# Forty zero matmuls from the start instead of fifteen later ones, a new order of all steps, and q loaded ahead of k, in a linear-attention and MLP-mixer kernel

## The chip, the cores and the metric

The kernel runs on one core of a Trainium2 chip. The metric is device time in microseconds (us). The core has a matrix engine (TensorE, PE in the profile; PEld are its weight loads), a vector engine (VectorE, DVE), a scalar engine (ScalarE, ACT), a general engine (GpSimd, POOL) and a sync engine (SyncE, SP) that issues almost all transfers. Each engine works off its own list of instructions in order; they wait for each other through semaphores. Transfers from SP are served by 16 DMA engines, behind each other in one queue (q1 in the profile); the ScalarE queue (q10) issues one load at the start and three stores at the end.

## The reference

Eight batches of eight heads, 576 tokens, 64 values per head. Linear attention with a cosine weighting of the position gives x, in which the heads stand side by side (512 channels); a token MLP (576 to 256 to 576) works across the tokens, and a channel MLP (512 to 1536 to 512) across the channels.

```python
def phi(x, c, s):
    r = np.maximum(x, 0.0)
    return np.concatenate([r * c, r * s], axis=-1)
q_p, k_p = phi(q, cos_w, sin_w), phi(k, cos_w, sin_w)
kv  = np.einsum('bhsf,bhsd->bhfd', k_p, v)
z   = np.sum(k_p, axis=2)
num = np.einsum('bhsf,bhfd->bhsd', q_p, kv)
den = np.einsum('bhsf,bhf->bhs', q_p, z)[..., None] + 1e-06
x   = num / den                                   # as [B, S, H * D]
xt  = x.transpose(0, 2, 1)
h   = np.maximum(xt @ w_tok1, 0.0) @ w_tok2
u   = x + h.transpose(0, 2, 1)
out = u + np.maximum(u @ w_ch1, 0.0) @ w_ch2
```

## The kernel before

The 576 tokens of a batch are 4.5 tiles of 128. Each partition pair holds nine consecutive tokens; five token slots j = 0..4 hold them, the last one half filled (the "tail"). The tails of two batches are worked on together as a ninth group. Matrix work is in bf16, with float32 sums in PSUM. There are two PSUM tiles of two banks each (psA, kind "P") and four of one bank (psM, kind "S"). A step that needs one takes the one that was freed longest ago, and its first write waits for the last reader of that tile.

The kernel is a list of steps, called one after the other; each appends its instructions to the lists of the engines. The order of the steps is therefore the order on every engine, and nothing is reordered later. These are the steps, with the profile's line for each:

- load_part, load (L272): q, k or v of a batch, in two parts (the tokens of the even and of the odd partitions), and for batch 0 v also by halves of the heads. One buffer each for q, k and v holds two batches' places but for one slot, so a load waits for the feature steps of the batch before. wtok_load (L461 to 465), wc1_load (L468), wc2_load (L488): the weights, as float32 into regions that are used for other things later (h1T, h1s, w_ch2t, u_sb, u_tl), and w1_cast, w2_perm, w2t_perm, wc1_cast, wc2_cast: to bf16.
- rfeat (L287, L289): relu of q. feat (L305 on ScalarE, L307 on VectorE): relu times cosine or sine for k, relu times tangent for q. vcast and vcast_half (L281, L283): v to bf16.
- q_turn_mm, q_turn_out (batches 0 and 1): eight transposes of q features on TensorE (L590) and the copy out of PSUM. q_turn (L319): the same for later batches, as a transposing DMA of SP.
- kv_half, kv_half_out, num_half, x_half, b1_half, b1_half_out (L506, L524, L539 to L548, L558): batch 0 in two halves of the heads. kv, kv_out, num, x_out, b1, b1_out (L603, L617, L624 to L627, L637): the other batches. x_half and x_out divide by the denominator, on VectorE.
- For batch 0, uT_x, uT_h, uT_out (L570, L575) make the transposed u on TensorE. For the others u_mm (L649), u_out (VectorE, L653), u_cast to bf16 and u_turn (L660), a transposing DMA of SP, make uT. u_sb has two buffers, so u_out of batch b overwrites what the store of batch b-2 reads. tail_mm, tail_out, tail_turn do this for the tails of two batches.
- m1 (L694), twelve of four matmuls for each group, and m1_out (relu into h1T, ScalarE L287 or VectorE L289). m2, m2_out (L706, L711): the second channel matmul of group 0. For the groups 1 to 8 it is done in seven block products instead of eight: h_sum (L348) and w_sum (L342) make sums of blocks of h1T and of w_ch2, prod (L359) multiplies, seed copies one PSUM bank into another, quarter (L371) adds a result to u_sb.
- store (L382, L383): two transfers for each half of the rows (0: slots 0 and 1, after the products 2 and 3; 1: slots 2 and 3); store8 for the tails.
- warm(n): n matmuls of a zero tile wz (128 columns of weights, 512 columns), into a bank that nothing reads (L496).

Before, the order comes from four tables of (place, step): ONCE for batch 0 and the weights, BATCH for the attention of batches 1 to 7, GROUP for the groups 1 to 8, where the table of a batch or group is repeated with its places moved on by 19 a batch. All are merged and sorted by place:

```python
steps(0, (), ONCE)
for b in range(1, B + 1):
    start = 19 * (b - 1)
    if b < B:
        steps(start, (b,), BATCH.get(b, BATCH["any"]))
    steps(start, (b,), GROUP.get(b, GROUP["any"]))
for _, _, fn, args in sorted(todo, key=lambda x: x[:2]):
    fn(*args)
```

Of the kernel before, what the change touches and what calls it, by code (L numbers as in the profile page):

```python
# [20 lines left out]
ONCE = (  # L21
# [15 lines left out]
    (-161.5, "vcast_half", 1, 0, "G"), (-103.1, "kv_half", 0, 0), (-151.6, "vcast_half", 0, 1, "G"),  # L37
    (-113.7, "vcast_half", 1, 1, "G"), (-102.6, "kv_half", 0, 1), (-151.4, "vcast_half", 0, 2, "G"),
    (-133.5, "vcast_half", 1, 2, "V"), (-95.2, "kv_half", 0, 2), (-110.7, "vcast_half", 0, 3, "A"),
    (-152.0, "vcast_half", 1, 3, "G"), (-94.5, "kv_half", 0, 3), (-116.5, "vcast_half", 0, 4, "V"),  # L40
    (-113.3, "vcast_half", 1, 4, "G"), (-87.2, "kv_half", 0, 4), (-72.2, "kv_half_out", 0, "A"), (-102.3, "warm", 3),
    (-63.4, "num_half", 0, 0), (-61.2, "x_half", 0, 0, 0), (-59.9, "x_half", 0, 0, 1), (-55.8, "num_half", 0, 1),
    (-51.9, "x_half", 0, 1, 0), (-51.7, "x_half", 0, 1, 1), (-61.0, "num_half", 0, 2), (-59.3, "x_half", 0, 2, 0),
    (-57.5, "x_half", 0, 2, 1), (-120.8, "kv_half", 1, 0), (-95.9, "kv_half", 1, 1), (-93.4, "kv_half", 1, 2),
# [141 lines left out]
def kernel(  # L186
# [570 lines left out]
    for b in range(1, B + 1):  # L757
        start = 19 * (b - 1)
        if b < B:
            steps(start, (b,), BATCH.get(b, BATCH["any"]))  # L760
        steps(start, (b,), GROUP.get(b, GROUP["any"]))
# [33 lines left out]
```

## Time and profile before

| what | value |
| --- | --- |
| median of three runs | 267.06 us (267.02 to 267.6) |
| span of the profiled execution | 265.7 us |
| TensorE busy | 245.6 us, 2081 matmuls |
| VectorE busy | 186.4 us |
| ScalarE busy | 135.5 us |
| GpSimd busy | 90.1 us |
| moved by DMA | 57.70 MB, mean 217 GB/s |
| TensorE's first matmul | 12.49 us |
| first m1 matmul | 33.13 us |

The span is that of one execution, taken by the hardware profiler. "Busy" is the time that an engine's instructions cover; the records of matmuls overlap, so that a busy TensorE is not one at its peak. The chain of waits is followed back from the last instruction, at each step to what released it. Its lines give start, length, engine, tile and line. A timeline line has start, length, engine, line, operation, operands, count, and in brackets the idle time before it and what ended that.

### The profile page before, as it was taken

To read this page: it belongs to the slowest core of one execution; us is meant where nothing else is said; L and a number is where in the kernel's file an instruction comes from. 1 tells how busy PE (TensorE), PEld (TensorE's weight loads), DVE (VectorE), ACT (ScalarE), POOL (GpSimd) and SP (SyncE) were. 2 spreads that over 40 slices of the span, in tenths; PEclk is the share of its full clock that TensorE was granted. 3 is DMA by queue.
4 is the path that set the end of the run, shared out by engine and by line. 5 is a ranking of instruction groups with operands and counts; after the bars stand their busy time and mean duration, and the time that the engine had idled before them with its cause. 6 is when DMAs were issued, how large, how long until landed. Compare 5 with 4: busy or idle time off the path is not lost.

```text
span 265.7 us, 5384 instructions
## 1 busy us (share of the span) xinstructions
PE 245.6 (92%) x2081; PEld 158.7 (60%) x2081; DVE 186.4 (70%) x360; ACT 135.5 (51%) x233; POOL 90.1 (34%) x109
## 2 busy tenths in 40 slices
PE   0198999998999999999999999999999999999993
PEld 0176556554448855775487548754875486486482
DVE  4468888969779879778695868587948384256462
ACT  2547678845754387448636863486324402521300
POOL 5064255609634106420460046006600240130340
PEclk9999999999999999999999999999999999999999
DMA  6999999799999899969999999996972043103004
GB/s 195 393 398 386 382 383 368 252 290 152 284 372 157 188 347 336 160 128 317 345 198 128 293 377 182 134 342 221 157 119 121 0 81 148 34 1 158 2 0 159
DMA packets 81754, 57.70 MB, mean 217 GB/s; under 512 B 50240, under 2 KB 76480, under 8 KB 81728
## 3 DMA queue, kind: packets, MB, share of 16 engines
q1 hardware_dynamic: 80768, 56.31, 76.6%
q10 hardware_dynamic: 960, 1.05, 1.3%
q8 instruction: 16, 0.26, 0.4%
q14 instruction: 10, 0.08, 0.1%
HBM read 35.85 MB, written 9.44 MB: 170 GB/s over the span
## 4 chain that ended last, share of the span: by engine, by line
PE 86%; DMA 6%; DVE 3%; SPq 1%; ACT 1%; issue 1%; POOL 1%; DVEq 0%; POOLq 0%
PE psM L694 35%; PE psM L359 26%; PE psA L637 6%; PE psA L649 5%; DMA uT<-u_bf 3%; PE psA L603 3%; DMA v_raw<-in_v_dram 3%; PE psA L617 3%; PE psM L706 2%; PE psM L496 1%; SPq L272 1%; PE psA L676 1%; PE psA L590 1%; PE psM L506 1%; DVE u_sb L653 1%
## 5 line engine op out<-in xcount | busy, mean ns | idle before, releaser
L694 PE MATMUL psM<-uT,w_ch 128*128 128x512 bf16 x384 | 89.9, 379 | 1.4 <-DMA uT<-u_bf 1.4
L287 ACT ACTIVATE h1T<-psM 128x512 bf16<-128x512 f32 x92 | 51.5, 596 | 55.9 <-PE psM L694 54.1
L694 PEld LDWEIGHTS <-w_ch 128*128 128x128 bf16 x432 | 40.5, 98 | 45.4 <-DMA uT<-u_bf 1.8
L283 POOL CAST vb<-v_raw 128x512 bf16<-128x512 f32 (+1 forms) x30 | 20.0, 698 | 70.5 <-DMA v_raw<-in_v_dram 70.5
L359 PEld LDWEIGHTS <-h1s 128*128 128x128 bf16 x384 | 36.7, 98 | 4.9
L371 DVE TENSOR_TENSOR u_sb<-psM,u_sb 128x512 f32<-128x512 f32 x42 | 28.7, 688 | 15.0 <-PE psM L359 14.7
L348 POOL TENSOR_TENSOR h1s<-h1T,h1s 128x512 bf16<-128x512 bf16 (+1 forms) x16 | 21.1, 1318 | 43.9 <-ACT h1T L287 31.3
L359 PE MATMUL psM<-w_ch2t,h1s 128*128 128x256 bf16 x288 | 34.4, 273 | 0.0
L359 PEld LDWEIGHTS <-h1T 128*128 128x128 bf16 x288 | 27.5, 98 | 4.8
L653 DVE TENSOR_TENSOR u_sb<-psA,x_sb 128x1024 f32<-128x1024 f32 x16 | 19.4, 1220 | 12.7 <-PE psA L649 12.5
L305 ACT ACTIVATE kp<-k_raw,sin_t 128x512 bf16<-128x512 f32 x32 | 22.3, 716 | 7.0 <-DMA k_raw<-in_k_dram 5.0
L359 PE MATMUL psM<-w_ch,h1T 128*128 128x256 bf16 x192 | 23.6, 273 | 0.0
L348 DVE TENSOR_TENSOR h1s<-h1T 128x512 bf16<-128x512 bf16 (+1 forms) x24 | 17.5, 728 | 5.5 <-ACT h1T L287 5.4
L305 ACT ACTIVATE kp<-k_raw,cos_t 128x512 bf16<-128x512 f32 x24 | 16.9, 716 | 6.2 <-PE psA L603 5.9
L627 DVE TENSOR_TENSOR x_sb<-psA,rden 128x512 bf16<-128x512 f32 x28 | 19.4, 691 | 1.0
L289 DVE TENSOR_SCALAR h1T<-psM 128x512 bf16<-128x512 f32 x16 | 10.8, 686 | 10.7 <-PE psM L694 10.4
L590 PE MATMUL psM<-ident,qp 128*128 128x128 bf16 x40 | 4.4, 274 | 12.5 <-ACT qp L287 12.5
L617 PEld LDWEIGHTS <-qpT 128*128 128x128 bf16 x280 | 12.3, 98 | 5.5
L649 PE MATMUL psA<-B,w_tok 128*128 128x512 bf16 x64 | 15.6, 379 | 0.0
L283 POOL CAST u_bf<-u_sb 128x1024 bf16<-128x1024 f32 x7 | 9.5, 1359 | 16.3 <-DVE u_sb L653 14.0
L624 DVE TENSOR_SCALAR rden<-psA,eps_t 128x8 f32<-128x8 f32 x35 | 7.8, 223 | 10.3 <-PE psA L617 9.3
L348 POOL TENSOR_TENSOR h1s<-h1T 128x512 bf16<-128x512 bf16 x8 | 10.1, 1261 | 13.3 <-ACT h1T L287 13.3
(114 smaller groups left out, 342.1 us busy)
## 6 DMA issues: line engine op xcount, KB each, us to landing
out_dram<-u_sb SPq DMA_DIRECT2D x32, 256.0 KB, 7.8
q_raw<-in_q_dram SPq DMA_DIRECT2D x8, 640.0 KB, 5.5
k_raw<-in_k_dram SPq DMA_DIRECT2D x8, 640.0 KB, 7.1
v_raw<-in_v_dram SPq DMA_DIRECT2D x7, 640.0 KB, 8.2
q_raw<-in_q_dram SPq DMA_DIRECT2D x8, 512.0 KB, 4.4
k_raw<-in_k_dram SPq DMA_DIRECT2D x7, 512.0 KB, 6.0
v_raw<-in_v_dram SPq DMA_DIRECT2D x7, 512.0 KB, 7.0
u_sb<-in_moe_w_ch_dram SPq DMA_DIRECT2D x2, 1024.0 KB, 10.1
```

The source lines that it names most:

```text
L283: eng.tensor_copy(out_ap, in_ap)
L287: eng.activation(out_ap, in_ap, AF.Relu)
L305: eng.activation(dst, src, AF.Relu, bias=0.0, scale=s)
L348: eng.tensor_tensor(out=o[:, k0:k1], in0=a[:, k0:k1], in1=b_[:, k0:k1], op=op)
L359: nc.tensor.matmul(bank[:, t * HC:(t + 1) * HC], lhs[:, ki, t * P:(t + 1) * P], rhs[:, ki, :], start=(first and ki == 0 and t == 0), stop= ...
L371: V.tensor_add(u, bank2(bank)[:, ts, :], u)
L617: nc.tensor.matmul(ps[:, h // HH, (h % HH) * E1:(h % HH + 1) * E1], qpT[:, h, j, :], kv_sb[:, h, 0:E1], start=True, stop=True, skip_group_ ...
L627: V.tensor_mul(dst.rearrange("p (g h d) -> p g h d", g=2, h=HH), n[:, :, :, 0:D], bcast(r, [[HH, 2], [1, HH], [0, D]]))
L637: nc.tensor.matmul(ps[:, mi, :], w1[:, j, mi * P:(mi + 1) * P], rhs, start=(j == 0), stop=(j == NJ - 1))
L649: nc.tensor.matmul(ps[:, half, :], w2[:, ki, 2 * c + half, :], B1[b % 2][:, ki, :], start=(ki == 0), stop=(ki == NT - 1))
L653: V.tensor_add(u_sb[b % 2][:, 2 * c:2 * c + 2, :], of(("u", b, c)), x_sb[:, 2 * c:2 * c + 2, :])
L694: nc.tensor.matmul(ps.rearrange("p (t k) -> p t k", k=P), wc1[:, ki, s * P:(s + 1) * P], src[:, :, ki, :], start=(ki == 0), stop=(ki == NC ...
```

## The change

Three things.

The memset of wz moves ahead of the other memsets of VectorE:

```diff
+    V.memset(wz, 0.0)
     V.memset(raw["k"][:, :, NJ, :], 0.0)
     G.memset(raw["q"][:, :, NJ, :], 0.0)
     load_part(0, "k", 1, A)
...
-    V.memset(wz, 0.0)
     V.memset(raw["v"][:, :, NJ, :], 0.0)
```

The four tables and the sort are replaced by one flat list, PLAN, in which every step of the program stands once, in the order in which it is called:

```diff
-    for _, _, fn, args in sorted(todo, key=lambda x: x[:2]):
-        fn(*args)
+    for name, *args in PLAN:
+        known[name](*[engines.get(x, x) for x in args])
```

The order itself is new throughout, and for many steps the engine (the letter A, V or G) is another one. Instead of warm(3) and warm(12) there are twenty warm(2). These are rows of PLAN that matter here: the opening, and three places further on.

```diff
+PLAN = (
+    ("load_part", 0, "q", 0, "Y", 0, 8), ("load_part", 0, "q", 1, "Y", 0, 8), ("rfeat", 0, "q", 0, 2, "A"),
+    ("feat", 0, "q", 1, 4, "V"), ("feat", 0, "q", 1, 3, "V"), ("load_part", 0, "k", 0, "Y", 0, 8),
+    ("feat", 0, "k", 0, 3, "A"), ("rfeat", 0, "q", 2, 4, "V"), ("warm", 2), ("rfeat", 0, "q", 4, 5, "V"), ("warm", 2),
+    ("load_part", 0, "v", 1, "Y", 0, 4), ("warm", 2), ("warm", 2), ("warm", 2), ("warm", 2),
+    ("load_part", 0, "v", 0, "Y", 0, 4), ("vcast_half", 0, 4, "G"), ("feat", 0, "q", 1, 2, "V"),
+    ("vcast_half", 0, 0, "G"), ("warm", 2), ("warm", 2), ("feat", 0, "k", 0, 4, "A"), ("warm", 2), ("warm", 2),
+    ("load_part", 0, "v", 1, "Y", 4, 8), ("load_part", 0, "v", 0, "Y", 4, 8), ("warm", 2), ("q_turn_mm", 0, 3, "S"),
+    ("warm", 2), ("warm", 2), ("feat", 0, "k", 0, 2, "A"), ("vcast_half", 0, 3, "G"), ("feat", 0, "k", 1, 3, "V"),
+    ("feat", 0, "q", 1, 0, "V"), ("feat", 0, "q", 1, 1, "V"), ("feat", 0, "k", 1, 1, "V"), ("warm", 2),
+    ("q_turn_out", 0, 3, "V", "S"), ("vcast_half", 0, 2, "G"), ("vcast_half", 1, 2, "G"), ("vcast_half", 1, 1, "G"),
+    ("feat", 0, "k", 1, 4, "A"), ("vcast_half", 1, 3, "G"), ("wtok_load",), ("vcast_half", 0, 1, "A"),
+    ("w1_cast", 4, 5, "G"), ("feat", 0, "k", 1, 2, "V"), ("w1_cast", 0, 2, "G"), ("feat", 0, "k", 0, 0, "A"),
+    ("feat", 0, "k", 1, 0, "V"), ("q_turn_mm", 0, 4, "S"), ("q_turn_out", 0, 4, "V", "S"), ("w2_perm", 0, "G"),
+    ("q_turn_mm", 0, 0, "S"), ("load", 1, "q", "Y"), ("q_turn_mm", 0, 1, "S"), ("warm", 2),
+    ("feat", 0, "k", 0, 1, "V"), ("q_turn_mm", 0, 2, "S"), ("q_turn_out", 0, 0, "V", "S"), ("w1_cast", 2, 4, "A"),
+    ("kv_half", 0, 0), ("warm", 2), ("kv_half", 0, 1), ("kv_half", 0, 2), ("q_turn_out", 0, 1, "V", "S"),
+    ("kv_half", 0, 3), ("wc1_load", 2), ("kv_half", 0, 4), ("warm", 2), ("kv_half_out", 0, "A"), ("w2_perm", 1, "G"),
+    ("vcast_half", 1, 0, "V"), ("kv_half", 1, 0), ("kv_half", 1, 1), ("vcast_half", 1, 4, "V"), ("num_half", 0, 2),
+    ("num_half", 0, 0), ("load", 1, "k", "Y"), ("warm", 2), ("q_turn_out", 0, 2, "V", "S"), ("warm", 2),
+    ("x_half", 0, 0, 0), ("x_half", 0, 0, 1), ("b1_half", 0, 0), ("x_half", 0, 2, 0), ("num_half", 0, 1),
...
+    ("feat", 1, "k", 0, 0, "V"), ("feat", 1, "k", 1, 3, "V"), ("wc1_cast", 3, "G"), ("u_out", 0, 0),
+    ("uT_out", 3, "A"), ("u_mm", 0, 1), ("u_out", 0, 1),
+
+    ("m1", 0, 11), ("feat", 1, "k", 1, 1, "A"), ("wc1_cast", 10, "A"), ("m1", 0, 8), ("feat", 1, "k", 1, 2, "V"),
...
+    ("feat", 1, "k", 0, 3, "A"), ("q_turn_mm", 1, 2, "P"), ("wc1_cast", 0, "V"), ("q_turn_out", 1, 0, "V", "P"),
+    ("vcast", 1, 0, "V"), ("q_turn_out", 1, 2, "V", "P"), ("m1", 0, 0), ("load", 2, "k", "Y"), ("m1_out", 0, 11, "A"),
...
+    ("b1", 4, 0), ("q_turn", 5, 0), ("vcast", 5, 1, "G"), ("m1", 3, 10), ("m1_out", 3, 9, "V"),
+    ("m1_out", 3, 11, "A"), ("rfeat", 5, "q", 2, 4, "V"), ("store", 2, 0, "Y"), ("b1_out", 4, 0, "A"), ("b1", 4, 1),
...
+    ("u_mm", 4, 0), ("kv", 5, 1), ("h_sum", 3, 2, 0, 2, "G"), ("load", 6, "k", "Y"), ("feat", 6, "k", 0, 1, "A"),
+    ("feat", 6, "k", 0, 2, "A"), ("feat", 5, "k", 1, 4, "V"), ("u_out", 4, 0), ("m1_out", 3, 10, "V"),
```

Before, SP's loads of batch 0 went out in the order q part 0, k part 0, v, q part 1, v, v, v, then the third block of w_ch1 and the token weights; k part 1 is issued by ScalarE ahead of them in both kernels. Now they are q part 0, q part 1, k part 0, v four times, the token weights, then batch 1's q, the third block of w_ch1 and batch 1's k.

More of the change, by code (lines that the diff above doesn't have):

```diff
@@ L14 @@
 ALU = mybir.AluOpType
-ONCE = (
[3 rows of a table removed]
-    (-206.9, "load_part", 0, "v", 0, "Y", 4, 8), (-59.4, "warm", 12), (-131.9, "wtok_load"),
[11 rows of a table removed]
[L37 to L44, printed above, removed]
[3 rows of a table removed]
-    (-36.1, "wc1_cast", 3, "A"), (-62.3, "num_half", 1, 0), (-52.5, "num_half", 1, 1), (-48.8, "num_half", 1, 2),
-    (-56.7, "x_half", 1, 0, 0), (-51.5, "x_half", 1, 1, 0), (-43.4, "x_half", 1, 2, 0), (-55.3, "x_half", 1, 0, 1),
[4 rows of a table removed]
-    (-31.7, "uT_h", 0), (-31.1, "uT_out", 0, "A"), (-34.1, "uT_h", 1), (-31.7, "uT_out", 1, "V"), (-40.3, "uT_x", 2),
-    (-39.5, "uT_x", 3), (-38.3, "uT_h", 2), (-36.4, "uT_out", 2, "A"), (-31.0, "uT_h", 3), (-30.1, "uT_out", 3, "A"),
[21 rows of a table removed]
-)
@@ L135 @@
-BATCH[3] = (
[5 rows of a table removed]
-    (-29.01, "vcast", 0, "A"), (-28.7, "kv", 0), (-17.3, "num", 0), (-15.0, "x_out", 0),
-    (-32.8, "feat", "q", 1, 1, "V"), (-23.5, "q_turn", 1), (-26.9, "vcast", 1, "G"), (-23.6, "kv", 1),
-    (-20.5, "num", 1), (-18.5, "x_out", 1), (-30.2, "feat", "q", 1, 2, "V"), (-25.5, "q_turn", 2),
-    (-29.14, "vcast", 2, "V"), (-23.5, "kv", 2), (-20.7, "num", 2), (-11.3, "x_out", 2),
-    (-23.1, "feat", "q", 1, 3, "V"), (-15.9, "q_turn", 3), (-28.24, "vcast", 3, "G"), (-23.3, "kv", 3),
-    (-14.56, "num", 3), (-13.9, "x_out", 3), (-32.2, "feat", "q", 1, 4, "V"), (-23.34, "q_turn", 4),
-    (-24.8, "vcast", 4, "V"), (-22.4, "kv", 4), (-11.8, "num", 4), (-9.5, "x_out", 4), (-22.4, "kv_out", "A"),
-    (-1.3, "x_tail", "V"), (-9.1, "b1", 0), (-6.5, "b1_out", 0, "A"), (-7.75, "b1", 1), (-6.4, "b1_out", 1, "A"),
-    (-6.1, "u_mm", 0), (-5.8, "u_out", 0), (-4.2, "u_cast", 0, "A"), (-1.5, "u_turn", 0), (-5.0, "u_mm", 1),
-    (-4.3, "u_out", 1), (-1.55, "u_cast", 1, "G"), (-1.34, "u_turn", 1), (-3.5, "tail_mm"), (-1.2, "tail_out", "G"),
-    (21.8, "tail_turn"), (-44.4, "load", "k", "Y"), (-34.5, "load", "v", "Y"), (-34.9, "load", "q", "Y"),
-)
@@ L154 @@
-GROUP = {}
-GROUP["any"] = (
[5 rows of a table removed]
-    (13.0, "prod", 7), (14.0, "prod", 6), (15.0, "prod", 4), (16.0, "prod", 5), (17.0, "prod", 2), (18.0, "prod", 3),
-    (13.4, "seed"), (10.21, "h_sum", 0, 0, 6, "V"), (13.36, "h_sum", 2, 0, 2, "G"), (12.1, "h_sum", 1, 0, 2, "V"),
-    (13.6, "h_sum", 2, 2, 4, "G"), (14.1, "h_sum", 1, 2, 4, "V"), (12.4, "h_sum", 2, 4, 6, "V"),
-    (15.0, "h_sum", 1, 4, 6, "G"), (15.44, "h_sum", 3, 0, 6, "V"), (13.9, "quarter", 7), (14.2, "quarter", 6),
-    (19.3, "quarter", 4), (17.9, "quarter", 5), (18.2, "quarter", 2), (22.8, "store", 1, "Y"), (21.3, "quarter", 3),
-    (23.02, "store", 0, "Y"),
-)
@@ L748 @@
     engines = {"A": A, "V": V, "G": G, "Y": SY}
-    todo = []
-    def steps(start, first, rows):
-        for place, fn, *args in rows:
-            args = [engines.get(x, x) for x in args]
-            todo.append((start + place, len(todo), known[fn], [*first, *args]))
-    steps(0, (), ONCE)
[L757 to L761, printed above, removed]
-    for _, _, fn, args in sorted(todo, key=lambda x: x[:2]):
-        fn(*args)
+    for name, *args in PLAN:
+        known[name](*[engines.get(x, x) for x in args])
     _ = tile, bass_utils
```

94 lines of the change are left out of this document (62 added, 32 removed), and 212 rows, old and new, of tables (BATCH, GROUP, ONCE, PLAN).

## The prediction

> **What bounds the kernel now.** I read the busy table first, then the chain that ended last, then windows and the timeline of the opening.
>
> ```profile
> PE 245.6 (92%) x2081; PEld 158.7 (60%) x2081; DVE 186.4 (70%) x360; ACT 135.5 (51%) x233; POOL 90.1 (34%) x109
> ...
> 5.67 7.35 DMA v_raw<-in_v_dram
> ...
> 15.95 1.28 PE psM L496 x3
> ...
> 18.55 0.85 PE psM L590 x8
> 19.61 0.45 PE psM L590 x8
> ...
> 21.12 2.59 PE psM L496 x12
> ...
> 33.13 2.59 PE psM L694 x12
> ...
> 59.17 1.23 DVE u_sb L653
> 60.42 1.05 ACT u_bf L281
> ...
> 61.72 4.39 DMA uT<-u_bf
> 66.16 2.76 PE psM L694 x12
> ...
> 261.32 0.42 DVE u_tl L371
> ```
>
> TensorE sets the time. The chain gives the pitch of its matmuls at full clock: 2.59/12 = 0.216 us with 512 columns, 1.31/12 = 0.109 with 256, 0.24/8 = 0.030 with 65, 0.45/8 = 0.056 for a transpose. The program has 638 + 692 + 640 + 96 of them beside the zeros: 137.7 + 75.5 + 19.4 + 5.4 = 238.1 us of real work, the same in both kernels. From the first m1 matmul (33.13) on, 226.4 of it is left; 33.13 + 226.4 = 259.6, and the last product ends at 261.3. So only 1.75 us are lost behind the opening, 1.14 of them in the wait for uT before 66.16. Behind the last product come 4.4 us of add, store and end.
>
> The opening is another matter. From TensorE's first matmul at 12.49 to 33.13 are 20.6 us with 11.6 of real work. The 15 matmuls of zeros take 1.28 + 2.59 = 3.9. The three in 1.28 go at 0.427 each, half pace, and so do the eight transposes in 0.85; a microsecond later eight take 0.45. The rest is waiting, for v (landed at 13.02) and what follows it.
>
> ```profile
> 8.69 0.88 DVE L307 TENSOR_SCALAR kp<-k_raw,cos_t 128x512 bf16<-128x512 f32 x2 [4.51 <-DMA k_raw<-in_k_dram]
> ...
> 10.79 0.88 DVE L307 TENSOR_SCALAR qp<-q_raw,tan_t 128x512 bf16<-128x512 f32 x2 [0.82 <-DMA q_raw<-in_q_dram]
> ...
> 14.98 1.29 DVE L283 COPY qpT<-psM 128x1024 bf16<-128x1024 bf16 x2 [0.64 <-PE psM L590]
> ...
> 13.00:23.00 10.00, 9.40 (x110) 7.18 (x109) 7.32 (x18) 6.44 (x12) 5.81 (x13) 1.00 1.05 394
> 23.00:33.00 10.00, 8.74 (x85) 5.75 (x83) 8.42 (x20) 5.92 (x11) 2.73 (x7) 1.00 1.08 384
> 33.00:58.00 25.00, 25.00 (x246) 14.31 (x244) 19.89 (x39) 18.55 (x33) 11.68 (x19) 1.00 0.98 334
> ```
>
> The windows list PE, PEld, DVE, ACT, POOL busy, clock, DMA share, GB/s. DMA runs at 0.38 to 0.39 MB a microsecond, its limit here, till past 50 us. VectorE is busy for 19.89 of 25 us behind the opening: it is the second limit.
>
> **The change, part by part.** *Zeros from the start.* Their memset (0.27 us) goes ahead of k's pad memset, so TensorE can begin near 1.3 us. 22 of the 40 stand ahead of the first transposes: about nine at 0.427, thirteen at 0.216, over by 8 us, while nothing has landed. They cost nothing. Of the other 18, six (1.3 us) stand between the transposes of tiles 3 and 4 under VectorE's feature work, twelve (2.6 us) in pairs among kv, num and b1. A pair also takes a PSUM bank and waits for its last reader: the pair behind q_turn 1 needs the bank of q_turn_out 3, the one behind kv_half(0,0) that of q_turn_out 0. VectorE's list, below, makes those copies just in time; if PE instead of VectorE sets the pace there, the pairs cost up to 2.6. I take 0.
>
> *Is the clock kept?* Between 8 and 10 us TensorE idles, and from 13 to 17 it waits often. If it fell to half pace, the work between 13 and 20 us would take 2 us more; I take 0, keep 2 for the range. [...]
>
> *q ahead of k on SP's queue.* The bytes ahead of v's last part stay the same, so v still lands at 13.0, part by part from 11.6. Before, q's second part (landed 10.77) had k and the first v part ahead. Now q is complete after 1.70 MB instead of k's 1.84 MB (8.69): 0.13 MB less, 0.35 us, so 8.35. k follows at 10.1. The token weights now directly follow v and land by 16.2, about 3 us earlier; then q of batch 1 (19), third w_ch1 block (22), k (25), the other w_ch1 blocks (30.5), v (33.5), w_ch2: each some 2 us or more ahead of its use worked out from the plan, at the same 0.39.
>
> *The opening, walked.* VectorE starts at 8.35 and is not done before the first normalisation. Ten features, five of 0.44 (0.88/2) alone and five of 0.55 beside POOL's casts, two relus of q (0.69, 0.42), five q_turn_out of 0.65 (1.29/2; two of these were ScalarE's), two half casts of 0.35: 10.0, so 18.4. Then x_half(0,0): 0.37 + 0.69, done 19.5 (before: 21.63). TensorE is ready for it: kv_half(1,0) goes at 17.4 to 17.8, num_half(0,0) ends by 18.4. From there, other x_halves 4.7 with 0.4 of waits for num: 24.6; last b1_half 0.22; b1_half_out on VectorE 0.69; uT_h 3, uT_x 2, uT_h 2 1.1; u_mm twice 1.73, with three uT_out of 0.58 on ScalarE beside it; hand-overs 0.25 (5 of some 0.05, as 26.58 to 26.62 in the chain): first m1 at 28.6. Bounds: 27.9 with no hand-over lost, 30.6 with the half pace. In the plan 226.9 of real work is left there, 0.45 more than before (one transpose block is later).
>
> [...] With 0.44 throughout, the sum would be 0.6 less.
>
> *Behind the opening.* All steps are reshuffled and 7.8 us of VectorE's records more than before stand ahead of m1 of batch 1 (55.1 against 47.3, each count times its row). VectorE's records overlap: rows sum to 199, busy is 186, factor 0.935. Up to u_cast(1,1) that is 44.8 us; 8.35 + 44.8 + 1.2 lost = 54.4, plus 4.65 for the transposing DMA: 59, and TensorE would be there at 28.6 + 32.3 = 60.9. It fits with 2 us to spare, where before it had some 9. So local lateness: wc1_cast 0 (VectorE) is done at 34.7 to 35.3 for an m1 due at 34.3: 0.7. Others like it: between 0 and 3, I take 0.7. The wait for uT of batch 1: before, 7.3 us from the last u_mm (58.86) to 66.16 with 6.15 of work in it; now 7.0 of work, and the cast is VectorE's 0.68 instead of 1.05: 0.4. What was lost elsewhere before, 0.6, stays.
>
> *Stores moved past loads on SP.* u_out(b) overwrites what store(b-2) reads. SP issues in order, and store(2,0) now stands behind load(5,v) and q_turn(5,0). Behind a waiting u_out on VectorE stand m1_outs, h_sums and x_outs, and TensorE's next m1 (for a PSUM bank) and products wait for these.
>
> ```profile
> DMA to landing us min/median/max: 8.1/9.5/9.6
> ```
>
> That is the stores issued at 147 to 150, behind loads. Real work between the last quarter of batch 2, rows 0 and 1, and u_out(4,0): 14.2 before, 10.0 now; for batches 3 and 5: 10.7 and 4.1. Quarter 0.69, VectorE's backlog 1, issues 1.2, landing 9.5 is 12.4, against 10.0 + 0.86 of u_mm: 1.5 late; batch 3 0.8; batch 5 stores into quiet queues (landings at 196 to 202 took 2.3 to 3.1) and fits. Some of it is hidden by the slack of 8 to 10 us from u_mm to m1; between 0 and 4.8 (batch 5 landing at 7.5 too), I take 0.7.
>
> Losses: 0.7 + 0.7 + 0.4 + 0.6 + 0.7 = 3.1. Span 28.6 + 226.9 + 3.1 + 4.4 = 263.0, against 265.7 of the profiled execution. The median shown, 267.06, stands 1.36 above that span; with the same 1.36: **264.4 us**, 1.0% faster.
>
> **Rivals.** *A, all of it kept:* the new order hides its waits as the old did, losses 0.7. 262.0. For: the old order lost only 0.6 besides the uT wait. Against: every margin above is thinner.
>
> *B, slower: VectorE becomes the bound between 8 and 61 us.* If its records don't overlap as much (47.9 instead of 44.8) and it idles for half of the 5.1 us that it idled between 33 and 58, uT of batch 1 comes at 8.35 + 1.2 + 47.9 + 2.55 + 4.65 = 64.7, 3.7 after TensorE is ready; 264.4 + 3.7 = 268.1, up to 270 with all 5.1. It decides when VectorE idles more than 2 us between 28 and 56. For: 98% load. Against: ahead of uT's deadline nearly nothing it needs comes late.
>
> *C, the opening gives less:* the clock falls to half pace, or the zeros' bank waits set TensorE's pace; first m1 at 30.6: 266.4. The change then doesn't do what it says. [...]
>
> *D, stores hold u_out* for batches 2, 3 and 5 and nothing hides it: 264.4 + 2.5 = 266.9. For: the 9.5. Against: before, the first of two uT halves had 10 us and more to spare.
>
> **How the numbers follow.** Forecast 0.48, A 0.20, B 0.14, C 0.08, D 0.10. The likeliest case's own range is 262.8 to 265.8. The range 261.0 to 268.4 leaves out A with a first m1 at 27.9 and less (0.06) and the upper half of B (0.08). About 0.2% is what a measurement of this kernel can tell from no change; that is 266.5 to 267.6. Faster: forecast, A, half of C, 0.72; within: halves of C and D, 0.09; slower: B and half of D, 0.19.
>
> **What would show it.** Right: zeros at 0.216 before 8 us, transposes of 0.45 from their first block, x_half(0,0) ended near 19.5, first m1 near 28.6, VectorE with few gaps from 8 to 56, short TensorE waits between m1 of batch 0 and 1. Wrong: a first m1 after 31, transposes at 0.85 behind the zeros, a TensorE wait of several microseconds for uT of batch 1 (B), u_out released by a DMA of out (D), or m1 waiting for w_ch1.

## The result, and the profile after

The kernel after takes 284.5 us (284.4 to 285.7), against 267.0 of the kernel before: 1.067 times as long, interval 1.0639 to 1.0701. The forecast was 264.4. Its profiled execution has a span of 283.9 us, against 265.7.

The page's busy table and the shares of the chain, and under them three lines of TensorE's timeline in the opening (start, length, engine, line, operation, shape, count, idle time before it and what ended that):

```profile
PE 257.8 (91%) x2106; PEld 160.7 (57%) x2106; DVE 210.3 (74%) x392; ACT 125.2 (44%) x208; POOL 96.8 (34%) x102
...
PE 56%; DVE 21%; DMA 10%; issue 5%; ACT 4%; SPq 1%; DVEq 0%; POOL 0%; ACTq 0%; POOLq 0%
...
1.19 7.22 PE L558 MATMUL psM<-wz 128*128 128x512 bf16 x22 [1.19 <-DVE wz L468]
9.79 0.62 PE L652 MATMUL psM<-ident,qp 128*128 128x128 bf16 x8 [1.37 <-DVE qp L351]
...
28.48 2.75 PE L756 MATMUL psM<-uT,w_ch 128*128 128x512 bf16 x12
```

The opening did what the change says: zeros over by 8.4 us, transposes at full pace from their first block (0.056 us apart), first m1 at 28.48 us instead of 32.97 (the timeline's start; the chain's 33.13 lies within the same group). 4.5 us are won. But VectorE now has 21% of the chain, and its busy time rose by 24 us. Summed record by record it is 27 us more, and at the old durations only 14 us of that would be work that came to it; the rest is the same operations taking longer. The last product ends at 279.8 instead of 261.3.

To see where, I take the times at which each group's first m1 starts, and subtract from each stretch the real matmul work that the plan has in it at full pitch:

```
first m1 of group    0      1      2      3      4      5      6      7      8
before            32.97  66.16  91.53 118.00 143.85 170.94 196.80 222.06 241.59
lost                  1.29   0.01   0      0      0.39   0.01   0      0     0.16
after             28.48  67.20  92.01 124.40 152.75 185.20 210.59 240.04 251.71
lost                  6.38   2.55   4.13   2.01   5.54   2.27   0.84   0     0.74
```

Behind the first m1 TensorE lost 1.9 us before and loses 24.5 now. With 0.45 us more work left there, 22.6 + 0.45 - 4.5 = 18.6: the 18.6 between 261.3 and 279.8. The gain is real; it is lost five times over, nearly everywhere in the body.

The chain of the kernel after shows two kinds of pieces that the chain before did not have, VectorE's copies from buffer to buffer, and waits for q: for its load, or for the transposing transfer (qpT<-qp) queued with it:

```profile
40.86 9.81 DMA q_raw<-in_q_dram
57.95 3.54 DVE u_bf L345
62.72 2.00 DVE u_bt L345
67.37 8.59 PE psM L756 x32
...
93.19 7.21 DMA qpT<-qp
...
122.01 5.83 DMA q_raw<-in_q_dram
```

A cast of u to bf16 took 0.68 us on VectorE in the kernel before; here one takes 3.54. GpSimd's and TensorE's timelines of the same stretch, and the granted clock behind it (windows: bounds, length, PE busy, clock, DMA share, GB/s):

```profile
57.85 6.58 POOL L404 TENSOR_TENSOR w_ch2t<-w_ch 128x1536 bf16<-128x1536 bf16 x2
64.39 3.27 POOL L404 TENSOR_TENSOR w_ch2t<-w_ch,w_ch2t 128x1536 bf16<-128x1536 bf16 x1
...
62.74 0.40 PE L679 MATMUL psA<-kv_sb,qpT 128*128 128x65 bf16 x8 [0.99 <-DVE u_tl L744]
65.87 0.40 PE L679 MATMUL psA<-kv_sb,qpT 128*128 128x65 bf16 x8 [1.87 <-DVE x_sb L689]
...
64.00:67.30 3.30, 0.74 (x18) 1.00 0.86 190
67.30:70.70 3.40, 3.40 (x12) 0.50 1.14 311
```

GpSimd's row of two w_sums has its seam at 60.94 and its end at 64.43; the two casts end 0.55 and 0.29 us behind these. Behind the casts in VectorE's queue stand u_tl and x_sb, on which TensorE waits; and after TensorE was busy for only 0.74 of 3.3 us, its clock is at half for 3.4 us, which costs 1.7 more.

### The profile page after: what moved, and what is told of

It is laid out like the page before. It is cut to its first block, busy times and chain, and to the rows that moved or that the text cites. A ratio compares the mean times of both kernels' runs of the same rounds, so it can differ in the third digit from the quotient of the medians.

```text
span 283.9 us, 5433 instructions
## 1 busy us (share of the span) xinstructions
PE 257.8 (91%) x2106; PEld 160.7 (57%) x2106; DVE 210.3 (74%) x392; ACT 125.2 (44%) x208; POOL 96.8 (34%) x102
## 3 DMA queue, kind: packets, MB, share of 16 engines
q10 hardware_dynamic: 960, 1.05, 1.2%
## 4 chain that ended last, share of the span: by engine, by line
PE 56%; DVE 21%; DMA 10%; issue 5%; ACT 4%; SPq 1%; DVEq 0%; POOL 0%; ACTq 0%; POOLq 0%
PE psM L756 25%; PE psM L421 19%; DMA q_raw<-in_q_dram 8%; PE psA L699 4%; PE psA L711 3%; DMA qpT<-qp 3%; DVE u_sb L715 2%; DVE h1s L410 2%; PE psA L679 2%; DVE kp L369 2%; DVE h1T L351 2%; DVE qp L369 1%; PE psA L665 1%; DVE u_bf L345 1%; DVE qpT L345 1%
## 5 line engine op out<-in xcount | busy, mean ns | idle before, releaser
L756 PE MATMUL psM<-uT,w_ch 128*128 128x512 bf16 x384 | 92.4, 384 | 3.6 <-ACT h1T L349 2.7
L349 ACT ACTIVATE h1T<-psM 128x512 bf16<-128x512 f32 x72 | 41.3, 595 | 77.3 <-PE psM L756 74.9
L410 POOL TENSOR_TENSOR h1s<-h1T 128x512 bf16<-128x512 bf16 (+1 forms) x18 | 29.3, 1642 | 56.6 <-ACT h1T L349 27.5
L351 DVE TENSOR_SCALAR h1T<-psM 128x512 bf16<-128x512 f32 x36 | 24.4, 685 | 8.1 <-PE psM L756 7.9
L345 POOL CAST vb<-v_raw 128x512 bf16<-128x512 f32 (+1 forms) x17 | 9.8, 600 | 48.8 <-DMA v_raw<-in_v_dram 48.2
L367 ACT ACTIVATE qp<-q_raw,tan_t 128x512 bf16<-128x512 f32 x23 | 16.0, 715 | 12.0 <-DMA q_raw<-in_q_dram 12.0
L679 PEld LDWEIGHTS <-qpT 128*128 128x128 bf16 x280 | 12.8, 99 | 11.2 <-issue 3.9
L679 PE MATMUL psA<-kv_sb,qpT 128*128 128x65 bf16 x280 | 14.0, 195 | 5.1 <-DVE x_sb L689 1.9
L349 ACT ACTIVATE qp<-q_raw 128x1024 bf16<-128x1024 f32 (+1 forms) x14 | 12.5, 900 | 11.0 <-DMA qpT<-qp 6.0
L410 DVE TENSOR_TENSOR h1s<-h1T,h1s 128x512 bf16<-128x512 bf16 (+1 forms) x17 | 15.3, 903 | 2.0 <-POOL h1s L410 1.9
L699 PE MATMUL psA<-x_sb,w_tok 128*128 128x512 bf16 x56 | 14.4, 379 | 1.5 <-DVE B L351 0.8
```

The source lines that it names most:

```text
L349: eng.activation(out_ap, in_ap, AF.Relu)
L351: eng.tensor_relu(out_ap, in_ap)
L367: eng.activation(dst, src, AF.Relu, bias=0.0, scale=s)
L410: eng.tensor_tensor(out=o[:, k0:k1], in0=a[:, k0:k1], in1=b_[:, k0:k1], op=op)
L679: nc.tensor.matmul(ps[:, h // HH, (h % HH) * E1:(h % HH + 1) * E1], qpT[:, h, j, :], kv_sb[:, h, 0:E1], start=True, stop=True, skip_group_ ...
L699: nc.tensor.matmul(ps[:, mi, :], w1[:, j, mi * P:(mi + 1) * P], rhs, start=(j == 0), stop=(j == NJ - 1))
```

## The experiments

Three theories. Theory 1: VectorE stands while GpSimd runs a tensor_tensor. Theory 2: VectorE has too much work, whatever its neighbour does. Theory 3: loads land late and hold up the in-order queues behind them. Beside these, the order alone: a step stands ahead of one that is needed sooner. "Lost" is worked out as above, up to the first m1 of group 2 (I) and behind it (II).

```
run          median  ratio to before (interval)   first m1  lost I  lost II
before       267.0                                  33.0      1.3     0.6
after        284.5   1.067  (1.0639 to 1.0701)      28.5      8.9    15.5
e1_open      269.3   1.0085 (1.0048 to 1.0123)      32.3      3.3     0.2
e1b_open     269.5   1.0101 (1.0053 to 1.0148)      28.4      9.0     1.0
e2_body      290.7   1.0899 (1.0858 to 1.0939)      33.2      8.4    14.9
e3_casts     281.5   1.053  (1.0488 to 1.0572)      28.2      7.8    12.7
e4_wsum      284.6   1.0637 (1.0574 to 1.0701)      28.4      7.8    15.9
e5_engines   296.5   1.1074 (1.1002 to 1.1146)      28.2     16.5    18.9
e6_engines   312.7   1.1708 (1.1655 to 1.1762)      32.3     20.8    28.1
e8_late      286.7   1.0732 (1.0694 to 1.077)       28.1      8.9    16.4
e9_hsum      281.8   1.0531 (1.0489 to 1.0573)      28.2      7.6    11.5
e10_graft    272.2   1.0167 (1.0125 to 1.0209)      28.2     10.1     1.2
e12_graft    272.0   1.0187 (1.0162 to 1.0212)      28.6     10.0     0.9
e11_nozero   287.9   1.077  (1.0721 to 1.0818)      28.6     10.5    17.3
f1_short     277.8   1.0393 (1.0369 to 1.0418)      28.1      8.8     8.3
f2_noload    279.1   1.0441 (1.0409 to 1.0472)      28.0      9.1    10.6
f3_both      271.8   1.0169 (1.014 to 1.0198)       28.4      8.6     2.5
f5_wsum      268.9   1.0067 (1.0042 to 1.0091)      28.4      5.1     2.5
f4_before    266.6   0.9974 (0.9958 to 0.999)       32.8      1.4     0.2
```

### Opening or body

e1_open and e2_body join the opening of one kernel with the order of the other; steps that the opening has done are skipped behind it (in e2_body q_turn_mm 1 of batch 1 also stays behind the first m1).

```diff
 e1_open
-PLAN = before
+PLAN = after[:first m1] + [s for s in before if s not in after[:first m1]]
 e2_body
-PLAN = after
+PLAN = before[:first m1] + [s for s in after if s not in before[:first m1]]
```

> Every step up to the first m1 as in the kernel after (22 early zeros, q ahead of k), all steps behind it in the order of the kernel before. Theory (the body's order is what cost the time, the opening is a gain): first m1 at 28.5 us against 33.0 before, and of these 4.5 us most stay, 262 to 264.5 us. Rival (the opening leaves casts and turns undone, and the rest has to pay for them, whatever its order): the m1 come early but the body loses more than it won, 266 to 275.

> The opening of the kernel before (first m1 at 33.0 us), all steps behind it in the order of the kernel after. Theory (the body's order costs it): the body loses some 20 us behind the first m1, as in the kernel after, 282 to 290 us. Rival (the debt of the new opening costs it): with the old opening the new order loses little, 267 to 274.

e2_body settles it for the body as a whole: the new order behind the old opening loses about as much as behind the new one (23.3 against 24.5) and takes 290.7 us. Behind group 2 the loss follows the order of the body: 14.9 us in e2_body, 0.2 in e1_open. Up to group 2 it is less plain, as e1b_open below shows.

e1_open is a miss: 269.3 us, and the first m1 came at 32.3. The old order puts q_turn_mm 1 of batch 1 ahead of the first m1, and TensorE stood there for its q features:

```profile
31.49 1.01 PE L642 MATMUL psA<-ident,qp 128*128 128x128 bf16 x8 [3.07 <-DVE qp L341]
```

e1b_open moves that one step behind four m1.

```diff
-    ("q_turn_mm", 1, 1, "P"), ("m1", 0, 8), ("m1", 0, 11), ...
+    ("m1", 0, 8), ("m1", 0, 11), ("m1", 0, 1), ("m1", 0, 2), ... ("q_turn_mm", 1, 1, "P"), ("m1", 0, 6),
```

> As e1_open, but q_turn_mm 1 of batch 1, which held TensorE for 3.2 us at 28.0 us ahead of the first m1, comes behind four m1. Theory (the opening is a gain that a body in the old order keeps): first m1 at 28.5, 262.5 to 264.5 us. Rival (the batch 1 features are late whatever the place, the wait only moves): 265.5 to 267.

The first m1 came at 28.4, and the next wait took it back: the third m1 wanted weights that GpSimd was to cast, and that the new order of loads brings later.

```profile
28.38 1.89 PE L746 MATMUL psM<-uT,w_ch 128*128 128x512 bf16 x8
34.87 1.64 PE L746 MATMUL psM<-uT,w_ch 128*128 128x512 bf16 x4 [4.60 <-POOL w_ch L335]
```

The loss was moved, not mended, and 269.5 us lies above the rival's range too. Up to group 2 both mixes lose much (9.0 us in e1b_open, 8.4 in e2_body, against 1.3 in the kernel before), so there a new opening in front of the old order costs time as well. An order and the loads ahead of it belong together.

### Sharing or order

e5_engines keeps the order of the kernel after and gives each step behind the first m1 to the engine that had it before; e6_engines is the converse.

```diff
-    ("m1_out", 0, 6, "V"), ... ("vcast", 1, 1, "A"),
+    ("m1_out", 0, 6, "A"), ... ("vcast", 1, 1, "G"),
```

> The kernel after, in its own order; behind the first m1 every step that VectorE, ScalarE or GpSimd can do runs on the engine that the kernel before gave it (some 186 steps change; VectorE's m1_out fall back from 36 to 16). Theory 2 (the new sharing of work loads VectorE): the body's 23.7 us of lost TensorE time fall to under 8, 263 to 271 us. Theory 3 (the order of the steps in each queue, whoever does them): the loss stays, 278 to 288. Theory 1 (stretched VectorE casts alone, 5 steps): the casts at 58, 62 and 117 us go from VectorE or not as the kernel before has them, so as with the five casts on ScalarE, 279 to 283.

> The converse: the kernel before, in its own order; behind the first m1 each of 175 steps is on the engine that the kernel after gave it. Theory 2 (sharing): 278 to 288 us. Theory 3 (order): 266 to 271. Theory 1: VectorE casts only stretch where they lie beside a tensor_tensor of GpSimd, which the old order need not have, 267 to 273.

Both are far slower than either kernel (296.5 and 312.7), outside the range of every theory. The gain that theory 2 foretold for giving VectorE's extra m1_out back to ScalarE didn't come; but both runs also pair all queues anew, so they don't refute it by themselves. f1_short, below, speaks against it more plainly: there VectorE's steps stay as they are and most of its loss goes with GpSimd's sums. My reading, not shown: the engine of a step was chosen for its place in its queue, and every queue is in order, so neither half is good or bad by itself.

### GpSimd beside VectorE, alone

```diff
+    for n in range(20):
+        G.tensor_tensor(out=dg, in0=halfg[:, :, 0:256], in1=halfg[:, :, 256:512], op=ALU.subtract)
+    for n in range(6):
+        V.tensor_copy(dv[:, 0, :], src[:, n, :])
+    for n in range(6):
+        V.tensor_scalar(dv[:, 1, :], src[:, n, :], scalar1=s1, scalar2=0.0, op0=ALU.mult, op1=ALU.max)
```

> Only measures: three times the same thirty VectorE operations (six each of: f32 to bf16 copy of 128x1024, the same of 128x512, the feature's tensor_scalar of 128x512, a bf16 tensor_tensor of 128x512, a relu from PSUM of 128x512), first with GpSimd idle, then beside GpSimd tensor_tensors of 128x1536 without a pause, then beside GpSimd f32 to bf16 copies of 128x1024. The output is not the reference's. Theory 1: the copies of 0.68 and 0.41 us take 1.5 to 4 us beside the tensor_tensors, and keep near their time beside the copies. Rival (a share of the access, the same for all): every form 1.2 to 1.6 times as long beside either.

In this run, which only measures, GpSimd's tensor_tensors and copies came in turn, and so did VectorE's 512 copies and features, so both neighbours are met in one stretch. First VectorE's lines with GpSimd idle, then beside it:

```profile
25.04 0.41 DVE L65 CAST dv<-src 128x512 bf16<-128x512 f32 x1
25.38 0.47 DVE L67 TENSOR_SCALAR dv<-src,s 128x512 bf16<-128x512 f32 x1
...
50.35 3.25 POOL L80 TENSOR_TENSOR dg<-halfg 128x1536 bf16<-128x1536 bf16 x1
50.59 3.30 DVE L67 TENSOR_SCALAR dv<-src,s 128x512 bf16<-128x512 f32 x1
53.55 1.23 POOL L84 CAST dc<-srcg 128x1024 bf16<-128x1024 f32 x1
53.81 1.25 DVE L65 CAST dv<-src 128x512 bf16<-128x512 f32 x1
54.74 3.25 POOL L80 TENSOR_TENSOR dg<-halfg 128x1536 bf16<-128x1536 bf16 x1
54.98 3.30 DVE L67 TENSOR_SCALAR dv<-src,s 128x512 bf16<-128x512 f32 x1
```

This is no share of a common rate. A feature of 0.47 us takes 3.30: it begins 0.24 us behind a tensor_tensor of 3.25 and ends 0.29 behind its end. VectorE's operation isn't done before GpSimd's is. The same is seen beside GpSimd's copies (0.41 to 1.25, beside one of 1.23, ended 0.28 behind it); there theory 1 expected no more than a little. What makes VectorE wait the trace doesn't show; how long, it does: 3.30 us beside 3.25.

In the kernel after itself, VectorE's operations by where they read, begun with no GpSimd tensor_tensor running, and begun while one ran:

```
                               none running            while one ran
reads SBUF: u_bf cast 1024     0.68 (kernel before)    2.74 mean of 3
            x_tc sum 512       0.41 (f1_short)         2.49
            h1s<-h1T sum 512   0.42 mean of 8          1.40 mean of 2
reads PSUM: h1T relu 512       0.685 mean of 28        0.685 mean of 8
            u_sb sum 512       0.685 mean of 40        0.682 mean of 6
```

What reads PSUM kept its 0.68 us in both columns. For the casts and sums, which read SBUF, it mattered who began first. In the kernel before, the casts of 0.68 us had GpSimd beside them as well, but each began 0.15 to 0.21 us ahead of a cast on GpSimd, and then it was GpSimd's that took longer, 1.37 to 1.43 us instead of the 1.04 that it takes alone:

```profile
135.49 0.68 DVE L283 CAST u_bf<-u_sb 128x1024 bf16<-128x1024 f32 x1
135.64 1.43 POOL L283 CAST u_bf<-u_sb 128x1024 bf16<-128x1024 f32 x1 [0.18 <-DVE u_sb L653]
```

The three casts of the kernel after (3.54, 1.51 and 3.18 us) all began while a GpSimd tensor_tensor was running.

### Mending single places

e3_casts gives the five casts to ScalarE, e4_wsum the three w_sums to VectorE, e9_hsum (on top of e3_casts) two h_sums of group 4 to VectorE; e8_late moves four steps of batch 4's q that I took to wait for its load.

```diff
 e3_casts
-    ("u_cast", 1, 1, "V"), ("tail_out", 1, "V"), ("u_cast", 2, 1, "V"), ("u_cast", 3, 0, "V"), ("tail_out", 3, "V"),
+    ("u_cast", 1, 1, "A"), ("tail_out", 1, "A"), ("u_cast", 2, 1, "A"), ("u_cast", 3, 0, "A"), ("tail_out", 3, "A"),
 e4_wsum
-    ("w_sum", 0, "G"), ... ("w_sum", 1, "G"), ("w_sum", 2, "G"),
+    ("w_sum", 0, "V"), ("w_sum", 1, "V"), ("w_sum", 2, "V"),
 e9_hsum
-    ("h_sum", 4, 0, 0, 6, "G"), ... ("h_sum", 4, 3, 0, 6, "G"),
+    ("h_sum", 4, 0, 0, 6, "V"), ... ("h_sum", 4, 3, 0, 6, "V"),
 e8_late
-    ("rfeat", 4, "q", 4, 5, "A"), ... ("feat", 4, "q", 1, 0, "A"), ... ("rfeat", 4, "q", 0, 2, "A"), ... ("q_turn", 4, 0),
     ("m1_out", 2, 9, "A"), ("m1_out", 2, 8, "A"),
+    ("rfeat", 4, "q", 4, 5, "A"), ("feat", 4, "q", 1, 0, "A"), ("rfeat", 4, "q", 0, 2, "A"), ("q_turn", 4, 0),
```

> The kernel after with the three u_cast and the two tail_out of VectorE on ScalarE, nothing else. Theory 1 (a VectorE cast from buffer to buffer is held up as long as GpSimd runs a tensor_tensor): the waits of TensorE at 62 to 67, at 120 and at 148 go, and with the first the half clock behind it; 4.0 + 1.7 + 0.9 us, so 277 to 280. Theory 2 (VectorE merely has too much work, the neighbour doesn't matter): only the five casts' own time at their short duration, 3 x 0.68 + 2 x 0.41 = 2.9 us, goes from VectorE, 281.5 to 283.5. Theory 3 (late loads and blocked queues set the body): 283.5 to 284.5.

> The kernel after with w_sum 0, 1 and 2 on VectorE instead of GpSimd, w_sum 0 moved to just ahead of w_sum 1. VectorE gets 3 x 0.95 = 2.9 us more work, GpSimd loses its 9.7 us. Theory 1 (GpSimd's tensor_tensor holds up VectorE): the casts at 58 and 62 us fall from 3.54 and 2.00 to 0.7 and 0.4 us, TensorE no longer waits there, 278 to 282.5. Theory 2 (VectorE has too much work): 284.5 to 287.5, longer than after. Theory 3 (late loads): 284 to 285.

> As e3_casts, and h_sum 0 and h_sum 3 of group 4 on VectorE instead of GpSimd: VectorE gets 2 x 0.95 us more work, GpSimd loses 2 x 3.09. Theory 1 (VectorE stands while GpSimd runs a tensor_tensor): the h_sum of 1.97 us at 167.6 and the x_tail of 2.49 us at 174.5 fall to 0.4 and 0.7, TensorE's waits of 0.6, 0.44 and 2.86 us behind them shrink; 2 to 4 us under e3_casts, 277.5 to 279.5. Theory 2 (VectorE has too much work): 1 to 2 us over e3_casts, 282 to 284. Order alone (who does it and beside what makes no difference): as e3_casts, 281 to 282.

> The kernel after; only the four steps of batch 4 that wait for its late q on ScalarE (two rfeat, one feat, the q_turn behind them) are put behind the m1_out of group 2 that they held up. Theory 3 (a load that lands late holds an in-order queue, and the m1_out behind it hold TensorE): the waits of 1.96 and 1.03 us at 102 to 106 go, 281.5 to 283. Rival (other work of the same batch is as late, the wait moves on to the kv or num of batch 4): 284 to 286.

e3_casts won 3.0 us: the lower end of theory 2's range, less than theory 1 foretold, so by itself it speaks for neither. e4_wsum and e9_hsum did to their casts and sums what theory 1 says (e4_wsum's casts took 0.69 and 0.43 us), yet won nothing in the median, against the kernel after and against e3_casts (by their times alone, 284.6 fits theories 2 and 3, and 281.8 the order alone): of e9_hsum's waits the one of 2.86 us went, and new ones of 1.98 and 2.10 us came nearby, as VectorE now did the sums itself. e8_late lost 2.1 us, near its rival's range, and so doesn't test theory 3: a vcast that waits for batch 4's v stayed ahead of the same m1_out.

```profile
102.54 0.62 ACT L332 CAST vb<-v_raw 128x512 bf16<-128x512 f32 x1 [6.72 <-DMA v_raw<-in_v_dram]
103.07 0.59 ACT L338 ACTIVATE h1T<-psM 128x512 bf16<-128x512 f32 x1
```

By now each single repair had handed its wait to the next step, so the causes had to be taken away whole.

### Taking the causes away

```diff
 f1_short, f3_both, f4_before, f5_wsum: in h_sum
-        eng.tensor_tensor(out=o[:, k0:k1], in0=a[:, k0:k1], in1=b_[:, k0:k1], op=op)
+        n_ = 8 if eng is G and g > 1 else TH
+        eng.tensor_tensor(out=o[:, k0:k1, 0:n_], in0=a[:, k0:k1, 0:n_], in1=b_[:, k0:k1, 0:n_], op=op)
 f2_noload, f3_both, f4_before, f5_wsum: in PLAN
-    ("load", 2, "k", "Y"), ... ("load", 7, "q", "Y"),
```

> The kernel after, GpSimd's h_sums of groups 2 to 8 over 8 of 256 columns each (the rest of the sums is left out), so that nearly all of GpSimd's tensor_tensor time behind 92 us goes while every wait for them stays. TensorE loses 15.5 us behind that place in the kernel after. Theory 1 (GpSimd holds up VectorE): 8 to 12 of these go, 272 to 277 us. Theory 3 (loads and queues): 2 to 4 go, 280 to 283. Order alone (a step stands in its queue ahead of one that is needed sooner): 1 to 3 go, 281 to 284.

> The kernel after without the loads of batches 2 to 7 (they compute with batch 1's rows; 18 loads are left out), so that no step waits for one and the DMA queues are near empty. Theory 1: the casts and sums stand as before, 281 to 284 us. Theory 3: the waits at 50, 65, 102 to 106 and 122 us go, 8 to 15 us, 270 to 277. Order alone: 280 to 283.

> f1_short and f2_noload together. Theories 1 and 3 together carry the loss: 268 to 272 us. Order alone, with neither: 278 to 283, as TensorE still waits on VectorE and ScalarE steps that stand behind others.

> The control: the kernel before with the same two things left out. TensorE loses 1.9 us there behind the first m1, so neither can win much: 264.5 to 267 us under every theory.

These kernels leave out work (sums, loads, or both), so they measure and are no candidates. f1_short wins 6.7 us and f2_noload 5.4; together 12.8, about their sum. Behind group 2's first m1 the loss falls from 15.5 us to 8.3, to 10.6, and with both to 2.5: two separate causes carry nearly all of it. Each alone fell short of what its theory foretold: 7.2 us of lost time went in f1_short instead of 8 to 12, 4.9 in f2_noload instead of 8 to 15, and the times lie just above the ranges; f3_both and f4_before came out as theories 1 and 3 said. The old order, with both left out, gains 0.26%: it had the same loads and most of those GpSimd sums (27 against 36, w_sums included), and, as I read it, in places where they held up little. One place, in the kernel after and then in f1_short:

```profile
173.58 3.09 POOL L410 TENSOR_TENSOR h1s<-h1T,h1s 128x1536 bf16<-128x1536 bf16 x1 [0.46 <-DVE h1s L410]
174.47 2.49 DVE L730 TENSOR_TENSOR x_tc<-x_tl,x_tl 128x512 bf16<-128x512 bf16 x1
179.14 1.11 PE L421 MATMUL psM<-w_ch2t,h1s 128*128 128x256 bf16 x8 [2.70 <-DVE u_sb L433]
```

```profile
170.01 0.27 POOL L400 TENSOR_TENSOR h1s<-h1T,h1s 128x48 bf16<-128x48 bf16 x1 [1.30 <-DVE h1s L400]
171.38 0.41 DVE L720 TENSOR_TENSOR x_tc<-x_tl,x_tl 128x512 bf16<-128x512 bf16 x1
```

An x_tail of 0.41 us stood for two; u_out, a feature and the adds behind it came late, and TensorE waited 2.70 us for a bank. In f1_short that wait is gone, and with it a stretch of half clock at 180.0 us. Shorter sums on GpSimd also end sooner, which no run holds apart; but behind 92 us the kernel after shows only one wait for a GpSimd result, 1.9 us of VectorE's, and none of TensorE's or ScalarE's. The other cause, in the kernel after: a step of ScalarE for batch 4's q waits for a transposing transfer, and the m1_out behind it in its queue hold TensorE. In f2_noload both waits are gone.

```profile
100.49 0.63 ACT L349 ACTIVATE qp<-q_raw 128x512 bf16<-128x512 f32 x1 [4.80 <-DMA qpT<-qp]
103.83 0.59 ACT L349 ACTIVATE h1T<-psM 128x512 bf16<-128x512 f32 x1
104.47 1.02 PE L756 MATMUL psM<-uT,w_ch 128*128 128x512 bf16 x4 [1.79 <-ACT h1T L349]
```

The step overwrites the buffer that this transfer, of batch 3, still reads. The transfer was issued at 93.19 behind the load of q in SyncE's queue and landed 7.2 us later; in f2_noload, without that load ahead, it took 3.45. The load itself had landed by 97.1. So f2_noload takes late loads and late transposing transfers away together, and doesn't hold them apart. f5_wsum takes away what was left of theory 1, the w_sums at 58 us, by the edit of e4_wsum on f3_both.

> f3_both, and w_sum 0, 1 and 2 on VectorE behind the casts at 58 and 62 us (as in e4_wsum), so that no tensor_tensor of GpSimd but three of group 1 is left at its length. TensorE loses 6.3 and 2.2 us in f3_both from the first m1 to 92 us. Theory 1 (GpSimd's w_sums hold up VectorE's casts there, and the half clock follows): 4 to 6 of these 8.5 go, 265.5 to 268 us. Order alone: 0 to 2 go, 270 to 272.

From f3_both another 2.8 us, 3.5 of lost time: the stretch up to group 1 loses 2.4 instead of 6.3, and its cast takes 1.05 us instead of 3.54 (0.68 in the kernel before):

```profile
57.44 1.05 DVE L331 CAST u_bf<-u_sb 128x1024 bf16<-128x1024 f32 x1
```

The median ended 0.9 us above theory 1's range. 7.5 us of TensorE's time stay lost, though f5_wsum kept full clock to the end of its products (1.00 from 28.4 to 267 us): behind the first m1 the trace has eight waits of 0.2 to 1.7 us for VectorE and ScalarE steps, 5.3 us together. I didn't split these further; that they are the price of the order alone is worked out by subtraction, and not shown.

### The zeros, and a version with both

```diff
-    ("warm", 2), (twenty times)
```

> The kernel after without any of its forty matmuls of zeros. If the zeros are what keeps the clock up in the opening: the first real matmuls run at half pace for some microseconds from 9.7 us, the first m1 comes 1 to 3 us later than 28.5, 285.5 to 287.5. If VectorE and the loads set the opening whatever TensorE's clock: first m1 at 28.5 within 0.5 us, 284 to 285.

Without zeros TensorE's first forty transposes take 4.45 us, 0.111 each instead of 0.056, it is granted half clock from 18.5 to 22.0 us, and the first m1 comes at 28.57, as with them (28.48, at full clock from 5.9 to 67.3 us). So here the zeros do hold the clock, and the opening's gain isn't theirs: what is left for it is the new order of the steps and q's earlier landing, which no run takes apart. That the kernel takes some 3 us longer, more than either theory allowed, comes from the body, with half clock at 66.3 to 73.2 and 107.3 to 110.7; why TensorE has the waits ahead of these was not followed up.

```diff
 e10_graft
-PLAN = after
+PLAN = e3_casts[:first m1 of group 1] + [s for s in before if s not in e3_casts[:first m1 of group 1]]
 e12_graft
-    ("load", 3, "q", "Y"), ... ("q_turn", 2, 3),
+    ("q_turn", 2, 3), ("load", 3, "q", "Y"),
```

> e3_casts up to the first m1 of group 1 (64.4 us in e3_casts, 66.2 in the kernel before), then the order of the kernel before, which at that place has the same steps done but ten small ones. Theory (the old order from there on loses nothing, wherever it starts from): 1.8 us off the kernel before, 264.8 to 266. Rival (the old order lives from a lead of loads and features that the new beginning doesn't have): 267 to 272.

> e10_graft with one step moved: q_turn 3 of batch 2, which SyncE issued at 63.95 us behind load 3 of q and on which TensorE waited until 70.5, stands ahead of that load. Theory (a transfer in the wrong place of an in-order queue): the wait of 3.5 us and the 2.7 us of half clock behind it go, 265.5 to 267.5. Rival (the queues are full, the turn lands late wherever it stands): 270 to 272.5.

The grafts were to keep the gain: e3_casts up to group 1, then the old order. In e10_graft TensorE waited for one q_turn that stood behind a load in SyncE's queue. e12_graft moved it, and that wait went, but the same load now came later and ScalarE, with the m1_out behind, waited for it:

```profile
70.63 0.72 ACT L357 ACTIVATE qp<-q_raw,tan_t 128x512 bf16<-128x512 f32 x1 [9.66 <-DMA q_raw<-in_q_dram]
...
72.50 1.02 PE L746 MATMUL psM<-uT,w_ch 128*128 128x512 bf16 x4 [3.58 <-ACT h1T L339]
```

272.2 and 272.0 us, both by the rivals' forecasts. Behind group 2 both lose about 1 us, as the old order does. No version here that does all the work beats the kernel before.

## Why the prediction was wrong

*Right: the bound and the opening.* "First m1 at 28.6": 28.48. "q complete at 8.35": VectorE starts at 8.64. "Ended near 19.5" for x_half(0,0): 18.73. Zeros "over by 8 us": 8.4, but eleven of them went at 0.427 and eleven at 0.216; "nine" and "thirteen" were my estimate, which no run shows. "226.9 of real work is left": the account above closes with it.

*Wrong: the sum of losses behind the opening, 3.1 us.* It measured 24.5. Three of its steps failed.

- "The cast is VectorE's 0.68 instead of 1.05." The 0.68 came from casts that began just ahead of GpSimd's, as shown above. Begun behind the start of a w_sum the cast took 3.54 and the tail's 2.00. I had the rows for it, 0.44 alone against a mean of 0.525 over the 21 q features of the kernel before, and read that as a tax of a fifth on some records. But 0.44 was half of a merged pair. One record by itself took 0.479 where no GpSimd operation was beside it, and the five that had one beside them 0.674 on average, from 0.47 to 0.90: the mean hid that a few paid much. It was a wait for what was left of the neighbour's operation (3.30 us beside 3.25 in e7_side), and the plan put these next to 3.1 us ones. It wanted a look, for each VectorE step that reads SBUF, at what GpSimd's list has beside it. Taking GpSimd's long operations away won 7.4 + 3.5 = 10.9 us of lost time, the half clock that followed some of the waits included.
- "All steps are reshuffled", and then only VectorE's list up to m1 of batch 1 was costed, and the stores. The loads of batches 2 to 7, the transposing transfers behind them in SyncE's queue and the ScalarE steps that wait for either were not looked at: 4.8 us of lost time by f2_noload alone, 13.5 - 7.4 = 6.1 with f1_short's cause gone. "What was lost elsewhere before, 0.6, stays" is where these should have stood.
- "I take 0, keep 2 for the range." That was said of the clock in the opening, and there it held: full clock from 5.9 to 67.3 us. The 0 was a choice, not shown by the profile before. The step that failed is that the sum had no term for the clock in the body, where TensorE was busy for 0.74 of 3.3 us, with a longest gap of 1.87, and half clock followed for 3.4 us, 1.7 us of cost; behind a wait of 2.70 us it came again at 180.0.

*"Stores", 0.7, and rival D:* no. store(2,0), priced at 9.5 us, landed in 4.8 us at most, ahead of the step it could have held; the median of all is 2.5, the longest 7.3, and no long wait ended with one.

*Rival B* had the side and the place right: between 28.5 and 57.95 VectorE was busy for 23.8 of 29.45 us, more idle than the 2 us from which B was to decide, and uT of batch 1 landed at 64.2 and 65.4, near B's 64.7. But TensorE's waits there were for VectorE's u_tl, x_sb and x_tl, not for uT, and B's price came from idle time and record overlap, up to 270. VectorE had not too much work: from 8.64 us to the cast at 57.95 it was busy for 41.3 us, less than the 44.8 forecast, and idle for 8.0. The cast, forecast to be done at 54.4, was done at 61.5; of these 7.1 us 2.9 are its own stop and the rest waits ahead of it. f5_wsum, with the same VectorE list up to the cast (57.44), lost 4 us less up to group 1, so there the stop beside GpSimd decided. And B ended at 61 us, where 18 of the 24.5 us were still to come. Rival C did not happen. A, everything kept, was the furthest off.

The mistake under all three: I costed the places that I had found, and gave the rest of a new order the losses of the old one. An order without losses is the rare case; e5_engines and e6_engines show what an untuned pairing costs (35 and 49 us lost).

## What to carry to other kernels

Before trusting a VectorE duration, see what GpSimd runs at that time: here the casts, features and sums that read SBUF, and began while a GpSimd tensor_tensor ran, ended only behind its end (3.30 us instead of 0.47 beside one of 3.25), and everything queued behind them paid too, while a cast that began 0.15 us ahead of GpSimd's kept its 0.68 us; put such a step on ScalarE, or give GpSimd's long tensor_tensors places where VectorE works from PSUM. When an order is replaced as a whole, cost every in-order queue to its end, loads included, since a repair at one place mostly hands the wait on. A gain ahead of a tight pipeline is kept only if the loads come earlier as well.

## What the runs showed of the hardware

- VectorE and GpSimd: a wait for the other's end, not a slower pace (0.47 to 3.30 us beside a 3.25 us tensor_tensor, 0.41 to 1.25 beside a 1.23 us copy); in the kernel after, VectorE operations that read PSUM kept 0.685 us with and without a tensor_tensor beside them. A VectorE cast that began 0.15 us ahead of GpSimd's kept its 0.68 us, and GpSimd's took 1.43 instead of 1.04. VectorE's reciprocals of 128x8 read SBUF too, and kept 0.20 us inside a tensor_tensor (at 64.89 and 65.98 us, beside one of 3.27 that began at 64.39). Beside VectorE's operations in e7_side GpSimd's copy took 1.23 to 1.50.
- The clock: ahead of its last product the kernel after was granted half pace twice, for 3.41 us at 67.32 and at 179.96. In the 3.41 us ahead of these TensorE was busy for 0.85 us (25%, from 63.91) and 0.82 us (24%, from 176.55), and the longest waits there were 1.87 and 2.70 us. From 101.46 to 104.88 it was busy for 1.63 us (48%), with a longest wait of 1.79, and kept full clock. In e11_nozero half pace lasted from 18.5 to 22.0, from 66.3 to 73.2 and from 107.3 to 110.7 us. From what busy time or gap on the clock falls, these runs don't show. The busy times rest on modelled ends of matmuls, and some traces lack a few matmul records.
